# Attention scan with MoE on one core: another fixed table for the order of each engine's instructions

## The chip, the cores and the metric

The kernel runs on one core of one Trainium2 chip. The metric is the device time of one execution in microseconds (us). Five engines have an instruction queue of their own and work through it strictly in its order: TensorE (PE, with its weight loads PEld), VectorE (DVE), ScalarE (ACT), GpSimd (POOL) and SyncE (SP). SP issues every transfer (DMA) of this kernel. Where one engine needs another's result, or a transfer's, it waits at that instruction, and everything behind it in its queue waits too.

## The reference

Two stages. The first is a linear recurrence over 768 steps for 4 batches, 8 heads and 48 x 48 states, with a complex decay; the second is a feed-forward layer on 3072 tokens, 384 to 2048 and back.

```python
scale = np.minimum(mag, 0.999) / (mag + 1e-06)        # mag = |a|
for t in range(S):
    new_re = ar * S_re - ai * S_im
    new_im = ar * S_im + ai * S_re
    S_re, S_im = (new_re + k_t v_t^T, new_im)
    y[:, :, t] = q_t . S_re
h = x @ w_in                                          # x: y, heads side by side
g = h * np.tanh(softplus(h))
return g @ w_out
```

## The kernel before

The tokens are cut into 12 units of 256 (three to a batch, since the state S runs on from unit to unit within a batch), and each unit into two chunks of 128. A unit goes through three kinds of work.

- **Elementwise** (`ew_steps`, lines 341 to 530): the decays' magnitudes and angles are turned into running products. Tiles R and I hold the decay's real and imaginary part (loads at L358), QK holds q and k (loads at L365), X and X1 are work tiles. ACT squares, takes logarithms, exponentials and sines (L258 is a helper that records most of its operations, L278 the sines and L266 the change of its function table). DVE multiplies: L484 is QK times X, and the two at L505 write QK and X, which SP then turns into the tiles T (L501, twelve transfers a unit).
- **Attention of a chunk** (`attn_steps`): from unit 3 on, DVE transposes T into the tile vx (L586), SP writes vx to HBM as kd (L590), waits for that to land, and reads it back as three pieces of the tile kn (L592). PE then computes pd (L656) from kn and V, and DVE adds pd to the state S (L663, L664). PE computes the scores pa (L609), DVE masks them into am (L612, L616), and PE sums ypsum (L636) from am, V, vx, T and S. ACT copies ypsum to y (L641) and SP moves y into the layout of the second stage (xf, L690). There is one tile kn and one tile vx; V has two buffers.
- **Feed-forward** (`moe_steps`): 100 steps. In each, PE computes ph (L723, 18 matmuls), ACT makes exponentials and squares of it (e, L258), DVE clips (L728) and multiplies (g, L733), g is split into gh and gl (L290, L291), and PE accumulates po (L760, 12 matmuls). The results leave through o (L773, L775) and a write to out_dram (L776). The weights are converted and split in the first 165 us (raw, w). Lines L719 and L756 are the same two products for the first half steps. `spin` (L548) records 84 matmuls on junk data at the start.

What sets the order: nothing is left to a scheduler. `ORDER`, from line 74, holds one string of numbers for each of PE, Activation, Pool and SP, and one for DVE. The numbers count an engine's instructions in the order in which the program records them; `24+3` stands for 24, 25, 26. `in_order` ties each instruction to the one named before it. The buffers of every tile are handed out in the order of recording, so the tables don't touch them.

A number behind a name (X_2242) is that of the tile: R_1638, I_1639, X_2242, QK_2291 belong to unit 5, R_2243, I_2244, X_2817 to unit 6; kd4_1 is kd of unit 4, chunk 1.

Of the kernel before, what the change touches and what calls it, by code (L numbers as in the profile page):

```python
# [75 lines left out]
        0+24 40+4 48+8 44+4 56+8 24+8 64+16 32+4 124+4 36+4 128+8 80+12 188+3 226+3 92+4 248+3 191+3 229+3 136+4 251+3  # L76
        96+8 156+16 140+16 172+8 286+3 180+8 104+4 210+16 194+16 289+3 294+3 232+4 292+2 236+8 297+3 108+8 302+6 244+4
        254+32 116+4 300+2 310+6 308+2 318+3 120+4 321+3 316+2 326+18 324+2 348+9 344+4 368+9 357+9 377+9 366+2 408
        386+22 412+4 410 409 416+13 411 443 442 445 438+4 502+16 444 446+9 429+9 455+9 473 464+8 476+8 518+4 472 474
        484+18 522 475 530+18 568+9 523 526+4 524 577+9 525 606+9 560+8 586+8 548+6 615+9 557+3 597+3 636+9 554+3  # L80
        645+9 594+3 600+6 666+18 627+3 624+3 630+6 696+9 654+9 726+9 663+3 705+9 684+3 744+8 764+8 735+9 690+3 687+3
        693+3 714+6 776+9 720+6 755+3 834+18 785+9 752+3 761+3 825+3 758+3 822+3 831+3 896+18 828+3 950+9 868+6 959+9
        877+3 874+3 938+12 968+6 980 977+3 981+17 974+3 772 798+24 773+3 852+8 794+4 860+8 1018+18 998 880+16 914+24
        1001+3 999+2 1007+3 1047 1004+3 1044+3 1050+3 1048+2 1082+3 1010+8 1036+8 1088 1053+3 1085+3 1091+3 1056+18
        1102+9 1089+2 1111+9 1156+6 1144+3 1162+3 1147+3 1153+3 1185+3 1165+9 1202+9 1191+3 1211+5 1150+3 1216+4
        1182+3 1188+3 1120+24 1074+8 1094+8 1174+8 1240+18 1220+3 1226+3 1302+9 1266+3 1272+2 1194+8 1232+8 1278+24
        1258+8 1274 1223+3 1311 1229+3 1269+3 1275+3 1312+8 1332+18 1370+9 1323+3 1320+3 1326+3 1379+9 1350+3 1329+3
        1353 1356+2 1354+2 1408+18 1358+12 1400+8 1388+6 1397 1446+7 1508+9 1394+3 1453+11 1517+5 1398 1426+3 1399
        1432 1429+2 1522 1433+2 1431 1523+3 1472+3 1435+3 1554+9 1478+2 1475+2 1563+9 1477 1480+4 1584+9 1484+24
        1438+8 1464+8 1526+8 1546+8 1537+3 1534+3 1593+9 1540+2 1543+3 1542 1602+8 1622+8 1572+6 1630+9 1581+3 1578+3  # L90
        1639+9 1610+12 1648+2 1651 1660+18 1650 1654+3 1698+9 1652+2 1707+9 1657+3 1736+9 1681+3 1678+3 1745+9 1690+8
        1716+8 1687+3 1774+9 1828+3 1684+3 1831+4 1724 1835+2 1727+3 1725+2 1783+5 1730+3 1758+3 1837+5 1874+8 1788+4
        1733+2 1842+2 1735 1882 1761+3 1767+3 1764+3 1883 1844+2 1792+24 1884+3 1816+3 1887+5 1819+5 1825+3 1857
        1912+4 1858+2 1824 1754+4 1846+8 1770+4 1866+8 1916+5 1863+3 1854+3 1921+9 1860+3 1904+8 1950+24 1930+8 1974+9
        1892+9 1983+3 1901+3 1941+3 1986+6 1938+3 1947+3 1995+3 2004+18 2042+18 1944+3 2001+3 2025+3 2031+11 2060+8
        1992+3 2080+18 1998+3 2126+9 2071+3 2022+3 2135+9 2028+3 2068+2 2077+3 2180+8 2070 2188 2109+2 2074+3 2106+2
        2111 2108 2189+2 2098+8 2144+24 2198+8 2191+3 2112+2 2226+9 2194+4 2218+8 2118+8 2114 2235+7 2168+3 2174+3
        2115+3 2242+2 2206+3 2171+3 2264+9 2177+3 2209+3 2215+2 2273+9 2212+3 2217 2326+2 2256+8 2282+8 2328+7 2244+3
        2250+3 2290+3 2335+5 2247+3 2296+3 2253+3 2340+4 2293+3 2299+3 2356+17 2344+3 2350+3 2347+3 2373 2394+18
        2353+3 2374+6 2432+9 2383+2 2470+7 2385 2477+2 2441+9 2380+3 2479+5 2302+24 2386+8 2424+8 2412+5 2418+2 2417  # L100
        2420+4 2532+9 2453 2541+9 2484+4 2450+3 2454+2 2459+3 2456+3 2578+18 2508+24 2550+8 2462+8 2570+8 2488+11
        2502+3 2499+3 2505+3 2608+9 2558+3 2564+3 2561+2 2654+9 2626+8 2646+8 2563 2567+3 2596+3 2617+9 2602+3 2663+2
        2634+2 2665+7 2636 2599+3 2605+3 2640+3 2672 2637+3 2684+9 2643+3 2693+9 2722+9 2675+3 2673+2 2731+9 2681+3
        2678+3 2760+9 2702+3 2708+2 2705+2 2710 2748 2707 2711+3 2751+2 2749 2769+9 2714+8 2740+8 2798+9 2753 2750
        2852+4 2807+9 2757 2856+3 2758+2 2859+2 2754+3 2861 2782+2 2862+6 2785+3 2784 2898+10 2868+2 2791+3 2788+3
        2843 2908+2 2816+24 2778+4 2794+4 2870+8 2890+8 2840+3 2844+2 2910+5 2846+6 2915 2878+3 2936+9 2881+9 2945+9
        2998+9 2974+24 2928+8 2954+8 2916+3 3007+9 2922+3 2919+3 2925+3 2965+3 3028+9 2971+3 2962+3 3037+9 2968+3
        3016+3 3022+3 3019+2 3066+9 3021 3075+9 3025+2 3046+2 3104+10 3048 3114+6 3052+2 3027 3049+3 3055+3 3054
        3120+2 3150+17 3058+8 3084+14 3101+3 3204+8 3098+3 3133+3 3130 3250+11 3131+2 3139+2 3212+3 3167 3141 3261+6
        3215+2 3136+3 3192+6 3201+3 3217+5 3233+3 3198+3 3122+8 3168+24 3142+8 3222+8 3267 3230+3 3236+6 3288+16  # L110
        3350+4 3304+2 3354+5 3268+6 3277+3 3317+3 3242+8 3280+8 3326+24 3306+8 3274+3 3314+2 3380+5 3323 3385 3316
        3359+2 3324+2 3361+7 3320 3418 3371 3386+3 3419 3372+2 3389 3321+2 3390+8 3368+3 3420+4 3374+3 3398+3 3377+3
        3401+3 3424+3 3407+3 3427 3439 3404 3428+6 3405+2 3440+2 3434+5 3445+3 3410+8 3448+9 3494 3442+3 3474 3457+7
        3477+3 3475+2 3464 3495+2 3480+2 3465+9 3497+2 3556+7 3483+3 3482 3563+2 3499+13 3565+9 3520+6 3532+24 3486+8
        3574+8 3512+8 3594+8 3526+6 3602+2 3582 3604 3585 3632+5 3583+2 3586+2 3637+4 3605+6 3588+3 3678 3641 3611+8
        3591+3 3620+3 3619 3642+8 3626+3 3623+3 3679+5 3629+3 3684+3 3658+3 3687+9 3650+8 3670+8 3664+3 3696+3 3708+3
        3661+2 3702+3 3711+6 3738+8 3663 3746 3667+3 3699+3 3726 3717+2 3747+9 3719+7 3727+2 3732+3 3768+5 3705+3 3729
        3756 3773+4 3757+2 3762+3 3730+2 3735+3 3777+5 3759+3 3765 3798 3766+2 3782+4 3799+17 3789+2 3786+3 3828+9
        3792+3 3791 3795 3837+9 3796+2 3858+12 3816+3 3870+6 3822+3 3888+14 3819+3 3846+3 3825 3852+3 3918+4 3826+2
        3849+3 3855+3 3876+3 3902+4 3882+3 3906 3879+3 3885+3 3907+5 3922+5 3915+2 3912+2 3927+9 3917 3948+9 3914  # L120
        3957+9 4044 3978+8 3939+3 3945+3 3986+10 3969+3 3936+3 3942+3 3966+3 3972+3 3996+3 3975+3 3999+11 4011+3 4010
        4017+3 4014+3 4020+9 4032+6 4029+3 4038+6
    """,
    "DVE": """
# [890 lines left out]
```

## Time and profile before

| | us |
|---|---|
| median of 3 runs | 604.12 |
| lowest and highest of them | 603.61, 605.97 |
| the profiled execution, own time | 601.38 |
| its span, first to last instruction | 599.6 |

The profiled execution is the fastest of the four, 2.74 us (0.45%) under the median. PE is busy for 555.0 us of the span, DVE for 480.8, ACT for 484.3. A busy figure counts the time from an instruction's start to its end; matmuls overlap, so a PE that is busy in a whole stretch may still have lost time there, for example to a lower clock. PEclk, the granted clock of TensorE, is 1.00 at 2.4 GHz and 0.50 at 1.2 GHz. A releaser, the work named behind an arrow, is inferred from the semaphore that came last by the profile: where the engine named had long been done, it was another.

### The profile page before, as it was taken

How to read it: one execution, taken by the hardware profiler on the slowest of the kernel's cores; microseconds unless marked ns; L12 is line 12 of the kernel's file. 1: busy time of each engine (PE TensorE's matmuls, PEld its weight loads, DVE VectorE, ACT ScalarE, POOL GpSimd, SP SyncE). 2: the span in 40 equal slices, each digit the busy share in tenths (PEclk: the TensorE clock that was granted, in tenths of full speed). 3: DMA queues.
4: the chain of work that ended last, by engine and by line, in shares of the span. 5: the costliest groups of instructions: out<-in, count | busy, mean ns of one | idle time of the engine just before them, and what ended most of it. 6: DMA issues, size and time to landing. Idle time of an engine off the chain costs nothing.

```text
span 599.6 us, 13309 instructions
## 1 busy us (share of the span) xinstructions
PE 555.0 (93%) x5254; PEld 513.8 (86%) x5254; DVE 480.8 (80%) x865; ACT 484.3 (81%) x753; POOL 38.2 (6%) x58
## 2 busy tenths in 40 slices
PE   0878999999989989999899999899999999999995
PEld 0457777899989979999899899799989999999995
DVE  6989899999988968889878797797788887553542
ACT  7988999999876977999879888798788887455661
POOL 2112313230000000000000010000000000000000
PEclk9989999999999998999999999999999999999998
DMA  8787857324544835515817506527626524201000
GB/s 296 234 269 186 308 158 211 134 53 131 162 131 128 223 103 164 155 39 152 227 35 187 170 5 181 156 47 192 156 63 159 172 81 123 79 26 28 14 14 32
DMA packets 68041, 80.71 MB, mean 135 GB/s; under 512 B 5604, under 2 KB 60132, under 8 KB 67972
## 3 DMA queue, kind: packets, MB, share of 16 engines
q1 hardware_dynamic: 67972, 79.80, 45.9%
q8 instruction: 43, 0.70, 0.5%
q14 instruction: 26, 0.21, 0.1%
HBM read 44.63 MB, written 11.40 MB: 93 GB/s over the span
## 4 chain that ended last, share of the span: by engine, by line
PE 45%; DMA 19%; ACT 13%; DVE 13%; SPq 5%; issue 3%; DVEq 0%; ACTq 0%
PE po L760 17%; PE ph L723 15%; DMA kn<-kd 6%; ACT e L258 5%; DMA kd<-vx 5%; PE ypsum L636 4%; ACT X L258 2%; PE pa L609 2%; SPq L501 2%; PE pd L656 2%; PE junk L548 2%; PE ph L719 2%; PE po L756 2%; ACT L266 1%; SPq L592 1%
## 5 line engine op out<-in xcount | busy, mean ns | idle before, releaser
L723 PE MATMUL ph<-xH,w 128*128 128x256 f32 x1104 | 226.7, 287 | 2.6 <-DVE g L733 2.6
L760 PE MATMUL po<-w,gh 128*128 128x384 f32 x704 | 205.1, 341 | 0.2 <-DVE o L775 0.2
L723 PEld LDWEIGHTS ph<-xH,w 128*128 128x128 f32 x1104 | 181.3, 190 | 6.5 <-DVE g L733 2.8
L723 PE MATMUL ph<-xL,w 128*128 128x256 f32 x552 | 156.2, 283 | 0.6 <-DVE xL L291 0.6
L258 ACT ACTIVATE e<-e 128x512 f32<-128x512 f32 (+1 forms) x200 | 120.1, 610 | 26.1 <-DVE e L728 24.4
L760 PEld LDWEIGHTS po<-w,gh 128*128 128x128 f32 x704 | 130.3, 190 | 3.3 <-issue 1.8
L760 PE MATMUL po<-w,gl 128*128 128x384 f32 x352 | 118.9, 339 | 0.0
L723 PEld LDWEIGHTS ph<-xL,w 128*128 128x128 f32 x552 | 105.0, 190 | 2.4 <-DVE xL L291 0.8
L258 ACT ACTIVATE e<-ph 128x512 f32<-128x512 f32 (+1 forms) x100 | 57.3, 574 | 38.3 <-PE ph L723 34.9
L733 DVE SCALAR_TENSOR_TENSOR g<-e,ph 128x512 f32<-128x512 f32 (+1 forms) x100 | 66.0, 661 | 25.3 <-ACT e L258 16.4
L258 ACT ACTIVATE e<-e,fifth 128x512 f32<-128x512 f32 (+1 forms) x100 | 70.1, 702 | 1.3
L760 PEld LDWEIGHTS po<-w,gl 128*128 128x128 f32 x352 | 66.7, 190 | 0.2 <-DVE gl L291 0.2
L728 DVE TENSOR_SCALAR e<-e 128x512 f32<-128x512 f32 (+1 forms) x100 | 41.0, 411 | 30.7 <-ACT e L258 29.7
L291 DVE TENSOR_TENSOR gl<-g,gh 128x512 fp32r<-128x512 f32 x88 | 59.8, 682 | 4.8 <-ACT gh L290 4.5
L266 ACT ACT_TABLE_LOAD x47 | 60.3, 1283 | 1.6 <-PEq L971 0.8
L636 PE MATMUL ypsum<-am,V 128*48 128x128 f32 x240 | 37.0, 276 | 2.8 <-DVE am L616 2.4
L548 PE MATMUL junk<-cmask 128*128 128x512 bf16 x84 | 22.7, 418 | 14.4 <-DVE I L464 14.4
L324 POOL TENSOR_TENSOR raw<-raw 128x768 int32<-128x768 int32 x16 | 28.0, 1749 | 86.9 <-DVE raw L322 25.1
L258 ACT ACTIVATE X<-R 128x768 f32<-128x768 f32 (+1 forms) x40 | 30.0, 764 | 4.1 <-POOL X L488 2.0
L636 PE MATMUL ypsum<-T,S 96*48 96x128 f32 x320 | 33.1, 278 | 0.0
L258 ACT ACTIVATE X<-X 128x768 f32<-128x768 f32 (+1 forms) x42 | 31.2, 748 | 0.2
L656 PEld LDWEIGHTS pd<-V,kn 128*32 128x32 f32 (+2 forms) x880 | 18.0, 115 | 14.6 <-DMA kn<-kd 8.2
(93 smaller groups left out, 801.3 us busy)
## 6 DMA issues: line engine op xcount, KB each, us to landing
T<-X SPq DMA_DIRECT2D x72, 129.0 KB
T<-QK SPq DMA_DIRECT2D x72, 129.0 KB
raw<-w_in SPq DMA_DIRECT2D x8, 768.0 KB
raw<-w_out SPq DMA_DIRECT2D x8, 768.0 KB
kd<-vx SPq DMA_DIRECT2D x15, 384.0 KB
kn<-kd SPq DMA_DIRECT2D x45, 128.0 KB
V<-v SPq DMA_DIRECT2D x12, 384.0 KB
out_dram<-o SPq DMA_DIRECT2D x24, 192.0 KB
```

The lines of the kernel that those rows point to most:

```text
L258: ins = nc.scalar.activation(out, in_, func, **kw)
L266: ins = nc.scalar.preload_act_table_set(name)
L291: leng(out=lo, in0=src, in1=h.bitcast(F32), op=ALU.subtract)
L324: nc.gpsimd.tensor_tensor(hi, hi, lo, ALU.add)
L501: nc.sync.dma_start(rows[cs * NJ + j], src[:, c, j])
L548: ins = nc.tensor.matmul(junk, cmask, cmask.unsqueeze(1).broadcast_to([P, 4, P]), start=True, stop=True)
L636: nc.tensor.matmul(py[64 * par:64 * par + D, i, :], lhs, rhs, start=n == 0, stop=first or n == 1)
L656: nc.tensor.matmul(pd[lo:hi, h, :], knat[:, at0:at0 + hi - lo], own(c, h), start=not on_pe, stop=True)
L723: nc.tensor.matmul(ph[:, a, :], rows_in(parts[j][:, wp], kt, a), st[xp][:, kt, :], start=n == 0, stop=n == 8)
L728: nc.vector.tensor_scalar_min(e, e, math.exp(20.0))
L733: nc.vector.scalar_tensor_tensor(g, e, 2.5, ph, ALU.subtract, ALU.mult)
L760: nc.tensor.matmul(po[t], gp[:, a, tsl], rows_out(parts[NPAIR + j][:, wp], a), start=j in starts and a == 0 and n == 0, stop=j + 1 in ends ...
```

## The change

The strings of `ORDER` are replaced by others, for all five engines. They come from another run of the search that made the first ones, with transfers taken to land later than before. No operation, tile, buffer or transfer is added, removed or changed: each engine has the same instructions. The same 100 steps of the feed-forward stage follow each other on PE in the same sequence. What moves are the steps of the other two stages against them, by a few places mostly, and the transfers against each other. Of PE's table the first line was and is

```diff
     "PE": """
-        0+24 40+4 48+8 44+4 56+8 24+8 64+16 32+4 124+4 36+4 128+8 80+12 188+3 226+3 92+4 248+3 191+3 229+3 136+4 251+3
...
+        0+24 40+4 48+16 44+4 24+8 64+16 32+4 124+12 36+4 80+4 136+4 84+8 188+6 226+3 92+4 248+3 96+4 229+3 251+3
```

The first place is in unit 4's second chunk, at 206 to 231 us of the trace of before. On ACT, the square of unit 6's decay (X_2817<-I_2244) stood ahead of the sines of unit 5 (X1_2241, R_1638, L278):

```order
L258 ACTIVATE X_2242<-R_1638 128x6x128
L266 ACT_TABLE_LOAD
L641 COPY y_2316<-ypsum_100 112x4x128
L258 ACTIVATE X_2817<-I_2244 128x6x128
L278 ACTIVATE X1_2241<-I_1639 128x768
L278 ACTIVATE R_1638<-I_1639 128x768
L278 ACTIVATE R_1638<-R_1638,halfpi_93 128x768
L266 ACT_TABLE_LOAD
L258 ACTIVATE e_2499<-e_2499 128x512
```

It now stands behind them, and behind the next step's exponentials:

```order
L641 COPY y_2316<-ypsum_100 112x4x128
L266 ACT_TABLE_LOAD
L290 CAST gh_2348<-g_2346 128x512
L278 ACTIVATE R_1638<-I_1639 128x768
L278 ACTIVATE X1_2241<-I_1639 128x768
L258 ACTIVATE e_2499<-e_2499 128x512
L278 ACTIVATE R_1638<-R_1638,halfpi_93 128x768
L266 ACT_TABLE_LOAD
L258 ACTIVATE e_2499<-e_2499,fifth_97 128x512
L258 ACTIVATE e_2499<-e_2499 128x512
L258 ACTIVATE e_2557<-ph_2538 128x512
L641 COPY y_2316<-ypsum_100 112x4x128
L258 ACTIVATE X1_2816<-X_2817,tiny_95 128x768
L258 ACTIVATE X_2817<-I_2244 128x6x128
```

Where it followed the first copy of y_2316 at once, twelve instructions now stand between that copy and it. On SP, at the same place, the load of q for unit 5 (QK_2291<-q) stood behind all three pieces of kn, and the load of I_2244 among them:

```order
L365 DMA QK_2291<-k 128x6x128
L590 DMA kd4_1_2429<-vx_1633 96x1024
L592 DMA kn_102<-kd4_1_2429 128x1x256
L358 DMA I_2244<-a_im 128x768
L592 DMA kn_102<-kd4_1_2429 128x1x256 x2
L365 DMA QK_2291<-q 128x6x128
L776 DMA out_0_dram<-o_2463 128x384
L776 DMA out_0_dram<-o_2460 128x384
```

Now:

```order
L590 DMA kd4_1_2429<-vx_1633 96x1024
L365 DMA QK_2291<-q 128x6x128
L365 DMA QK_2291<-k 128x6x128
L592 DMA kn_102<-kd4_1_2429 128x1x256 x2
L776 DMA out_0_dram<-o_2460 128x384
L592 DMA kn_102<-kd4_1_2429 128x1x256
L358 DMA I_2244<-a_im 128x768
L776 DMA out_0_dram<-o_2463 128x384
```

Both loads of QK have moved ahead of the pieces of kn, I_2244 behind them, and a write of o_2460 stands before the last piece.

The second place is on DVE in unit 3, where vx_1633<-T_1395 is the transpose for the first chunk:

```order
L291 TENSOR_TENSOR gl_1670<-g_1667,gh_1669 128x512
L291 TENSOR_TENSOR gl_1727<-g_1724,gh_1726 128x512
L733 SCALAR_TENSOR_TENSOR g_1811<-e_1805,ph_1786 128x512
L455 TENSOR_TENSOR I_1127<-I_1127,X1_1636 128x3
L728 TENSOR_SCALAR e_1900<-e_1900 128x512
L291 TENSOR_TENSOR w11_1630<-raw11_550,w11_1630 128x768
L773 SCALAR_TENSOR_TENSOR o_1866<-po_1616,back_1864 128x384
L773 SCALAR_TENSOR_TENSOR o_1869<-po_1617,back_1864 128x384
L586 STREAM_TRANSPOSE vx_1633<-T_1395 96x8x4x32
```

Now:

```order
L733 SCALAR_TENSOR_TENSOR g_1811<-e_1805,ph_1786 128x512
L291 TENSOR_TENSOR w11_1630<-raw11_550,w11_1630 128x768
L290 CAST gh_1669<-g_1667 128x512
L586 STREAM_TRANSPOSE vx_1633<-T_1395 96x8x4x32
L291 TENSOR_TENSOR gl_1670<-g_1667,gh_1669 128x512
L728 TENSOR_SCALAR e_1900<-e_1900 128x512
L773 SCALAR_TENSOR_TENSOR o_1866<-po_1616,back_1864 128x384
L290 CAST gh_1813<-g_1811 128x512
L291 TENSOR_TENSOR gl_1727<-g_1724,gh_1726 128x512
```

The two gl, the clip of e_1900 and both o have moved from ahead of the transpose to behind it.

The third place is on SP in unit 9, first chunk, around kd9_0 and its three pieces of kn:

```order
L590 DMA kd9_0_4952<-vx_1633 96x1024
L501 DMA T_4884<-QK_4541 16x8x258
L592 DMA kn_102<-kd9_0_4952 128x1x256 x2
L365 DMA QK_5086<-q 128x6x128
L592 DMA kn_102<-kd9_0_4952 128x1x256
L501 DMA T_4884<-X_4500 16x8x258
L358 DMA R_5042<-a_re 128x768
```

Now:

```order
L590 DMA kd9_0_4952<-vx_1633 96x1024
L365 DMA QK_5086<-k 128x6x128
L592 DMA kn_102<-kd9_0_4952 128x1x256
L365 DMA QK_5086<-q 128x6x128
L592 DMA kn_102<-kd9_0_4952 128x1x256
L358 DMA R_5042<-a_re 128x768
L376 DMA vx_1633<-v 64x2x192
L592 DMA kn_102<-kd9_0_4952 128x1x256
```

Four loads that stood behind the last piece of kn, or one ahead of it, now stand between the landing of kd and that piece.

## Rows read from the trace of the kernel before

**Rows 1.** The page: busy; clock in 40 slices; a group (busy us, mean ns).

```profile
PE 555.0 (93%) x5254; PEld 513.8 (86%) x5254; DVE 480.8 (80%) x865; ACT 484.3 (81%) x753; POOL 38.2 (6%) x58
PEclk9989999999999998999999999999999999999998
...
L291 DVE TENSOR_TENSOR gl<-g,gh 128x512 fp32r<-128x512 f32 x88 | 59.8, 682 | 4.8 <-ACT gh L290 4.5
```

**Rows 2.** Waits of PE: waiting line <- releaser: total us, times, longest us.

```profile
PE junk L548 <- DVE I L464: 14.4, 1, 14.4
PE pd L656 <- DMA kn<-kd: 8.3, 9, 1.5
PE pkn L577 <- DMA T<-QK: 5.4, 3, 2.4
...
PE ypsum L636 <- DVE am L616: 2.4, 1, 2.4
```

**Rows 3.** Stretches: us, busy us (instructions) by engine, PEclk, DMA share, GB/s.

```profile
165.00:180.00 15.00, 13.02 (x96) 12.11 (x98) 12.14 (x22) 11.08 (x18) 1.02 (x2) 1.00 0.45 132
...
285.00:300.00 15.00, 12.70 (x127) 12.30 (x125) 12.31 (x24) 12.00 (x17) 0.58 (x2) 0.96 0.80 223
```

**Rows 4.** Timeline of PE: start us, us, what, count [idle before <-releaser].

```profile
221.65 0.87 PE L656 MATMUL pd<-V,kn 128*32 128x48 f32 x46 [1.01 <-DMA kn<-kd]
...
225.30 0.66 PE L636 MATMUL ypsum<-am,V 128*48 128x128 f32 x2 [2.42 <-DVE am L616]
```

**Rows 5.** Timeline of DVE, same columns.

```profile
222.84 1.76 DVE L484 TENSOR_TENSOR QK<-QK,X 128x1536 f32<-128x1536 f32 x1 [5.31 <-ACT R L278]
```

**Rows 6.** Timeline of ACT, same columns.

```profile
213.15 0.84 ACT L258 ACTIVATE X<-R 128x768 f32<-128x768 f32 x1
...
218.82 0.85 ACT L258 ACTIVATE X<-I 128x768 f32<-128x768 f32 x1 [2.94 <-DMA I<-a_im]
```

**Rows 7.** Timeline of SP's queue: start us, us of the issue.

```profile
206.66 0.34 SPq L590 DMA_DIRECT2D kd<-vx  x1
212.79 0.57 SPq L592 DMA_DIRECT2D kn<-kd  x1
...
215.07 0.79 SPq L365 DMA_DIRECT2D QK<-q  x1
```

**Rows 8.** Stretches of 4 us, columns as in rows 3.

```profile
224.00:228.00 4.00, 2.70 (x15) 2.24 (x16) 3.88 (x7) 1.90 (x4) 0.00 (x0) 0.50 0.12 45
228.00:232.00 4.00, 4.00 (x21) 4.00 (x20) 3.92 (x6) 2.81 (x5) 0.00 (x0) 0.68 0.51 134
```

**Rows 9.** Timeline of PE, units 3, 6 and 9, columns as in rows 4.

```profile
178.26 0.27 PE L656 MATMUL pd<-V,kn 128*32 128x48 f32 x2 [0.62 <-DMA kn<-kd]
179.86 0.87 PE L656 MATMUL pd<-V,kn 128*32 128x48 f32 x44 [1.32 <-DMA kn<-kd]
...
297.90 0.24 PE L656 MATMUL pd<-V,kn 128*32 128x48 f32 x2 [1.22 <-DMA kn<-kd]
299.24 1.49 PE L656 MATMUL pd<-V,kn 128*32 128x48 f32 x46 [1.09 <-DMA kn<-kd]
...
434.40 0.88 PE L656 MATMUL pd<-V,kn 128*32 128x48 f32 x48
```

**Rows 10.** Timeline of DVE, unit 3, columns as in rows 4.

```profile
166.75 1.00 DVE L773 SCALAR_TENSOR_TENSOR o<-po,back 128x384 f32<-128x384 f32 x2
```

**Rows 11.** Timeline of SP's queue, unit 9, columns as in rows 7.

```profile
424.71 0.55 SPq L592 DMA_DIRECT2D kn<-kd  x1
...
426.02 0.53 SPq L592 DMA_DIRECT2D kn<-kd  x1
```

**Rows 12.** Chain of waits in order of time: start us, us, what.

```profile
248.91 3.83 DMA QK<-q
...
290.87 8.32 DMA kn<-kd
...
515.96 5.17 DMA kn<-kd
```

More of the change, by code (lines that the diff above doesn't have):

```diff
@@ L75 @@
     "PE": """
[47 rows of a table removed]
[46 rows of a table added]
     """,
     "DVE": """
[29 rows of a table removed]
[29 rows of a table added]
     """,
     "Activation": """
[23 rows of a table removed]
[23 rows of a table added]
     """,
     "Pool": """
-        12+2 0 8 1 11 2+3 9 5+2 14 10 15+7 23 22 24+6 7 31 33 32 54 30 35 34 36+4 41 40 42+4 47 46 48+2 51 50 52+2
+        0 10 1 5 2 8 3 9 11 4 7 6 14+2 13 16 12 17+5 23 22 24+6 31 33 32 30 34 36 38+2 35 37 41 40 42+2 45 44 47 54 46
+        48+2 51 50 53 52
     """,
     "SP": """
[13 rows of a table removed]
[13 rows of a table added]
     """,
```

221 rows, old and new, of the table ORDER are left out of this document.

## Prediction

> **What bounds the kernel now.** The page's busy table comes first: PE is busy for 93% of the span, DVE and ACT for about 80% [rows 1]. So the time is PE's work plus what PE loses, and since no operation is changed, a table can only win back losses or add new ones. The second view is the list of what PE waited for [rows 2]. Its longest entry, 14.4 us, is the start: PE has nothing to do until the first angles are made. Behind it stand pd waiting for the read-back kn (8.3 us in 9 waits), pkn for the relayed T (5.4 us in 3) and one wait of ypsum for am (2.4 us). These 16.1 us, and what the clock loses after them, are about all that an order can win; the same list is the place where a worse table would show.
>
> The third view is the stretches, to see where the losses sit. At 165 to 180 us PE is busy for 13.0 of 15 us, at 285 to 300 for 12.7 [rows 3]. The worst place is 220 to 232 us. There pd waits 1.01 us for kn, then ypsum 2.42 us for am [rows 4], and the granted clock is 0.50 in the 4 us that follow and 0.68 in the next four [rows 8]: the lower of the two levels, 1.2 GHz.
>
> The fourth view is each engine's timeline there, followed back from am. DVE idles 5.31 us ahead of L484 [rows 5], so am, which stands behind it, is late. The row names ACT's sine R as releaser, but L484 is QK times X: it doesn't read R, and X's last exponential ended at 213.15 + 0.84 = 213.99 [rows 6]. What L484 also reads is the load of q, issued at 215.07 [rows 7], 7.77 us ahead of L484's start. I take that load as the true cause. It was late because SP's queue stood still: kd was issued at 206.66, the first piece of kn, which waits for kd's landing, at 212.79 [rows 7], and the load of q stood behind all three pieces. ACT has a stall of its own there: its square of the next unit's I waits 2.94 us for the load of I [rows 6], which stood between the same pieces, and unit 5's sines queue behind that square.
>
> **The change, part by part.** All sums are made against the profiled execution's own 601.38 us. The median of the runs is 604.12, 2.74 above it; I assume that distance to stay and carry the differences over to the median.
>
> *Unit 4, chunk 1.* Both loads of QK now stand directly behind kd instead of one behind the pieces of kn. If kd is issued as late as 2 us after 206.66, the load of q goes out by 210, 5 us earlier than at 215.07. With the same 7.77 us it lands by 217.8. DVE was ready for L484 at 222.84 - 5.31 = 217.53, so its stall falls from 5.31 to some 0.3 us. PE asked for am at 225.30 - 2.42 = 222.88; am is made some 2.5 us behind L484's start (225.30 - 222.84), so at 217.8 + 2.5 = 220.3. The wait of 2.42 us goes. ACT's square moves behind twelve instructions, sines and exponentials among them, so its load's lateness holds up neither the sines nor the step's exponentials: its 2.94 us are off the chain, and cost nothing more unless the load comes over 7 us later than those twelve allow. The clock: it is low from PE's restart at 225.30 to about 230.6 (4 us at 0.50 [rows 8], then (1 - 0.68) x 4 / 0.5 = 2.6 us), so 5.3 us of work at half speed, 2.6 us lost. It fell right behind this wait, so I let it go with it. The wait of 1.01 us for kn I leave: the pieces now stand behind two loads, and the last one behind a write of o_2460. Sum -2.4 - 2.6 = **-5.0**; bounds 0 (below) and -6.0 (with the 1.01).
>
> *Unit 3, chunk 0.* pd waits 0.62 + 1.32 = 1.94 us for kn [rows 9]. On DVE two gl (682 ns each by the page's group [rows 1]) and both o (1.00 us together [rows 10]) move from ahead of the transpose to behind it: 2.4 us. DVE is busy throughout there, so the transpose, kd and kn come up to 2.4 us earlier, and the wait is gone. The gl and o that now come later feed products several steps on; if that cover were gone, their 2.4 us would come back as a wait of po. **-1.9**; bounds 0 and -1.94.
>
> *Units 8 and 9.* In unit 9 the last piece of kn went out at 426.02, with the second at 424.71 and one load between [rows 11]: 0.65 us an issue. Now three more issues stand ahead of it, so it goes out some 2.0 us later, at 428.0. A piece took 5.17 to 8.32 us to land [rows 12], which gives 433.2 to 436.3, and PE took up pd at 434.40 [rows 9] without waiting: a new wait of 0 to 1.9 us. The piece is behind large loads, so the upper row is nearer; I take 1.0. Unit 8 has the same pattern, with more cover ahead of pd: 0.5. **+1.5**; bounds 0 and 3.8.
>
> For these pieces there is also a rule. The rows show the issues 0.65 us apart and no more: what a load ahead of a piece costs it in the transfer engines isn't to be seen in them apart. The Trainium skill, "DMA: Bandwidth & Descriptors", section "Queues, rings and completion order", says that each transfer engine consumes the descriptors of a ring in ring order, and that SP owns one row of rings. By it a piece would wait for all bytes ahead of it; the sum by the rows is the -5.4 below, by the rule it is the second rival's.
>
> *Unit 6* waits 1.22 + 1.09 us [rows 9] at a clock that falls too. Transpose and pd move later by about the same there: 0, bounds -3.8 and +1. *The other waits* for kn are 8.3 - 1.01 - 1.94 - 2.31 = 3.0 us, and pkn's 5.4 us belong to the first units, which alone use it and where the junk matmuls change places with the work: 0 for both, bounds -3 and +3, since I can't sign them by rows.
>
> Sum: -5.0 - 1.9 + 1.5 = **-5.4**: 601.38 - 5.4 = 596.0 in a profiled execution, 604.12 - 5.4 = **598.7** for the median.
>
> **The rivals.**
>
> *First: kn takes the wait that am leaves.* At the worst place PE stood at pd from 221.65 - 1.01 = 220.64, with the last pieces issued by 215.03. With two loads ahead (1.3 us) and the write of o_2460 to be waited for, the last one may go out 2.5 us later; pd then waits 3.5 us, the clock falls as before, and the 2.4 us of am are paid at pd instead. For it: SP's queue is strict, and DVE makes o_2460 only after other work. Against it: pd itself moves behind more products of the feed-forward stage. It gives 0 - 1.9 + 1.5 = -0.4: 603.7.
>
> *Second, the other side: loads ahead of kn are paid by their bytes.* A load of 384 KB takes 393 / 223 = 1.76 us at the 223 GB/s of a crowded stretch [rows 3]. In unit 9 two more stand ahead of the last piece (+3.5 us), in unit 8 three more (5.3, half of it covered: +2.6), in unit 4 two (+3.5, less am's 2.4: +1.1). One more fall of the clock, 2.6 us, comes with unit 9's wait. Sum 3.5 + 2.6 + 1.1 + 2.6 - 1.9 = +7.9: 612. It decides from the point where a piece takes longer than the 8.32 us that is the longest here. For it: 8.32 us stands for a piece behind loads, 5.17 us for one late in the kernel. Against it: a QK load alone took 3.83 us [rows 12], and in a queue that isn't full loads and pieces overlap. The page named above stands beside this one; it would make it the rule in every unit, and the rows' 8.32 against 5.17 bears it out only in part.
>
> *Third: the change doesn't do what it says.* The pieces might land no later than the first search assumed, the extra cover might fall on waits that weren't there, and each gain be matched by a new miss: 604.
>
> **How the numbers follow.** Forecast 0.58, first rival 0.24, second 0.13, third 0.05. The forecast's own range is 594.5 to 601. For 8 in 10 the range goes from 592.5, where unit 6, its clock and half of the unsigned waits go too (-5.4 - 3.8 - 2.4), to 607, which takes in the first and third rivals with 3 us of new waits and leaves the second out. About 0.5%, 3.0 us, is what a measurement of this kernel can tell from no change: faster than 601.1 has the forecast's 0.58, within has 0.29 (first and third), slower than 607.1 has 0.13.
>
> **What would show it.** In the new trace L484 of unit 5 starts without an idle time over 1 us, ypsum in unit 4 has no wait for am, and the granted clock between 210 and 240 us stays at 1.00. pd in unit 3 doesn't wait. In units 8 and 9 pd waits for kn by under 2 us each. A list of PE's waits with more than 8.3 us for kn speaks for the second rival; a pd wait of some 3 us near 222 us for the first. What would make the prediction wrong at once is a wait of PE of several us where before it had none, since PE is busy for 93% of the span and has no slack to pay it from.

## The result and the profile after

The changed kernel takes 579.16 us (median of four runs, 576.64 to 579.75), beside 603.87 us for the kernel before (602.16 to 605.97): a ratio of 0.958, interval 0.954 to 0.962. That is 24.7 us, where 5.4 were forecast, and it lies outside the range. The profiled execution took 578.97 us, with a span of 577.0. Medians and extremes, here and below, are over all runs; the ratios leave out the runs more than 1.5% above the fastest of their kernel.

The page of after, busy time and granted clock [rows 1]:

```profile
PE 547.6 (95%) x5254; PEld 509.5 (88%) x5254; DVE 480.8 (83%) x865; ACT 482.6 (84%) x753; POOL 39.7 (7%) x58
...
PEclk9899999999999999999999999999999999999999
```

The work is the same, the span shorter: PE's idle time fell from 44.6 us (599.6 - 555.0) to 29.4, and its busy time by 7.4 us. Part of that is the clock, which in this profile no longer drops between the start and the last matmul. It isn't all: with the order of before in all but one row, and no drop at all while PE works (e1_q_early, below), PE is still busy for 550.6 us, 3.0 more than here. What PE waited for, after [rows 2]:

```profile
PE junk L548 <- DVE I L464: 14.7, 1, 14.7
PE pd L656 <- DMA kn<-kd: 3.0, 3, 1.5
PE pkn L577 <- DMA T<-QK: 2.2, 2, 1.8
PE ph L723 <- DVE g L733: 1.2, 2, 0.8
```

Nine waits of pd for kn have become three, and the wait of ypsum for am (L616) is gone. Stretches of after [rows 3]; the middle one covers unit 4's second chunk:

```profile
165.00:180.00 15.00, 15.00 (x177) 14.23 (x178) 14.54 (x28) 12.99 (x20) 0.62 (x4) 1.00 0.34 109
210.00:225.00 15.00, 15.00 (x168) 14.50 (x168) 13.32 (x20) 14.38 (x22) 0.00 (x0) 1.00 0.52 141
285.00:300.00 15.00, 15.00 (x239) 14.12 (x238) 14.09 (x25) 13.61 (x22) 0.41 (x2) 1.00 0.31 103
```

PE is busy throughout, at the full clock. To see where the time went, PE's **loss** is followed along its work: the time less the sum of all matmuls so far, each at the usual distance between two starts at full clock (0.120 us in L723, 0.173 in L760; those of the small matmuls are estimates from the same traces, so a stretch can come out a little under zero). The stretches hold the same amount of PE's work in all kernels and are named by the time in the trace of before. "Mean" is over the profiles of this study with that order in that stretch. Some grafted orders (below) have their seam, where one order takes over from the other, inside a stretch and are counted there: at 184 us in unit 3 of after, at 268 in unit 4 and at 318 in unit 6 of before. The run that takes the order of before up again behind unit 3 (h_u3_only, loss 3.3) isn't in the mean of unit 4. Differences are taken before rounding.

| loss, us | before | after | mean, order of before | mean, order of after | difference of means | forecast |
|---|---|---|---|---|---|---|
| start, to 77 | 12.5 | 8.9 | 12.0 (10 profiles) | 10.5 (7) | -1.4 | 0 |
| to 160 | 3.3 | 3.8 | 3.3 (9) | 3.4 (6) | +0.1 | 0 |
| unit 3, to 212 | 2.3 | -0.4 | 2.7 (7) | -1.0 (7) | -3.7 | -1.9 |
| unit 4, to 289 | 6.7 | -0.3 | 6.3 (7) | -0.3 (4) | -6.6 | -5.0 |
| unit 6, to 334 | 4.3 | -0.8 | 3.4 (7) | -0.6 (5) | -3.9 | 0 |
| units 7 and 8, to 388 | 4.5 | 1.8 | 4.7 (9) | 2.3 (6) | -2.3 | +0.5 |
| the rest | 0.8 | -0.4 | 0.9 (11) | -0.6 (5) | -1.6 | +1.0 |

The means add up to -19.4 us. The whole change measured 24.7 in the first comparison and 21.4 in a second one (below). Some 1.2 us of the other 2 to 5 lie behind PE's work, where this loss doesn't look: from the start of PE's last matmul to the end of the span it takes 7.3 to 7.5 us in every profile that ends in the order of before, 5.9 to 6.4 in those that end in the order of after. The remaining 1 to 4 us aren't placed.

### The profile page after: what moved, and what is told of

It reads as the page before. It is cut to its first block, busy times and chain, and to the rows that moved or that the text cites. A ratio compares the mean times of both kernels' runs of the same rounds, so it can differ in the third digit from the quotient of the medians.

```text
span 577.0 us, 13326 instructions
## 1 busy us (share of the span) xinstructions
PE 547.6 (95%) x5254; PEld 509.5 (88%) x5254; DVE 480.8 (83%) x865; ACT 482.6 (84%) x753; POOL 39.7 (7%) x58
## 4 chain that ended last, share of the span: by engine, by line
PE 52%; DMA 6%; DVE 5%; SPq 3%; ACT 2%; issue 1%; DVEq 0%; ACTq 0%
PE po L760 22%; PE ph L723 21%; PE ypsum L636 4%; PE pa L609 3%; DMA kn<-kd 3%; PE pd L656 2%; SPq L501 2%; DMA kd<-vx 2%; ACT e L258 1%; DVE X L505 1%; DMA out_dram<-o 1%; DVE gl L291 1%; SPq L592 1%; DVE g L733 1%; ACT X L258 1%
## 5 line engine op out<-in xcount | busy, mean ns | idle before, releaser
L723 PE MATMUL ph<-xH,w 128*128 128x256 f32 x1104 | 225.7, 287 | 1.2 <-DVE g L733 1.2
L760 PE MATMUL po<-w,gh 128*128 128x384 f32 x704 | 202.3, 339 | 0.0
L723 PEld LDWEIGHTS ph<-xH,w 128*128 128x128 f32 x1104 | 180.7, 190 | 4.9 <-PE po L760 1.1
L723 PE MATMUL ph<-xL,w 128*128 128x256 f32 x552 | 156.0, 283 | 0.0
L258 ACT ACTIVATE e<-e 128x512 f32<-128x512 f32 (+1 forms) x200 | 119.7, 610 | 21.4 <-DVE e L728 19.6
L760 PEld LDWEIGHTS po<-w,gh 128*128 128x128 f32 x704 | 128.9, 188 | 2.4 <-issue 1.3
L760 PE MATMUL po<-w,gl 128*128 128x384 f32 x352 | 118.6, 337 | 0.8 <-DVE gl L291 0.7
L723 PEld LDWEIGHTS ph<-xL,w 128*128 128x128 f32 x552 | 104.7, 190 | 1.7 <-issue 0.6
L760 PEld LDWEIGHTS po<-w,gl 128*128 128x128 f32 x352 | 66.2, 188 | 1.4 <-DVE gl L291 1.3
L728 DVE TENSOR_SCALAR e<-e 128x512 f32<-128x512 f32 (+1 forms) x100 | 40.5, 409 | 16.5 <-ACT e L258 16.2
L548 PEld LDWEIGHTS <-cmask 128*128 128x128 bf16 x84 | 8.6, 106 | 23.9 <-issue 18.4
```

Of the source, the lines that this page charges most:

```text
L258: ins = nc.scalar.activation(out, in_, func, **kw)
L548: ins = nc.tensor.matmul(junk, cmask, cmask.unsqueeze(1).broadcast_to([P, 4, P]), start=True, stop=True)
L723: nc.tensor.matmul(ph[:, a, :], rows_in(parts[j][:, wp], kt, a), st[xp][:, kt, :], start=n == 0, stop=n == 8)
L728: nc.vector.tensor_scalar_min(e, e, math.exp(20.0))
L760: nc.tensor.matmul(po[t], gp[:, a, tsl], rows_out(parts[NPAIR + j][:, wp], a), start=j in starts and a == 0 and n == 0, stop=j + 1 in ends ...
```

## The experiments

Each ratio is to the kernel before on the same chip, with its 95% interval. For grafted orders "before until 188" means everything that had started by then in the trace of that kernel. There is one profile to a kernel: those of e1_q_early, e2_u6_pieces_first and b_pieces_first are of their fastest run, those of a4_q_late, a6_bulk_in_window and after_again of their slowest, so a loss read from one of them is not that of a typical run.

**The two loads in SP's queue, each alone.** First the load of q in unit 4:

```diff
 L590 DMA kd4_1_2429<-vx_1633 96x1024
+L365 DMA QK_2291<-q 128x6x128
 L592 DMA kn_102<-kd4_1_2429 128x1x256
...
-L365 DMA QK_2291<-q 128x6x128
```

> The kernel before, with one row of SP's queue moved: unit 5's load of q goes out directly behind the write of kd of unit 4, chunk 1, ahead of the three pieces of kn and the load of I; nothing else changes. My theory (the late load of q is what held am, 2.42 us of waiting and 2.6 us of low clock behind it): the load goes out near 207.0 instead of 215.07, L484 idles under 1 us instead of 5.31, the wait for am is gone, 599 to 601.5 us. Rival (kn takes the wait: the pieces go out behind one more load, pd waits 2 to 3.5 us instead of 1.01 and the clock falls as before): 603 to 605 us.

600.26 us, ratio 0.998 (0.9945 to 1.0019; ten runs from 593.74 to 603.88): no verdict by time. The trace shows the mechanism. L484 of unit 5 in this kernel [rows 5], on DVE, and then pd on PE [rows 4]:

```profile
215.73 1.76 DVE L484 TENSOR_TENSOR QK<-QK,X 128x1536 f32<-128x1536 f32 x1
```

```profile
219.61 0.87 PE L656 MATMUL pd<-V,kn 128*32 128x48 f32 x46 [0.63 <-DMA kn<-kd]
```

L484 has no idle time ahead of it, ypsum doesn't wait for am, pd waits no longer than before, and unit 4's loss is 3.0 instead of 6.7. The reverse is clearer, since the runs of after lie closer together. The kernel after with that row put back:

```diff
 L590 DMA kd4_1_2429<-vx_1633 96x1024
-L365 DMA QK_2291<-q 128x6x128
 L365 DMA QK_2291<-k 128x6x128
...
 L592 DMA kn_102<-kd4_1_2429 128x1x256
+L365 DMA QK_2291<-q 128x6x128
 L358 DMA I_2244<-a_im 128x768
```

> The kernel after, with one row of SP's queue put back: unit 5's load of q goes out behind the three pieces of kn of unit 4, chunk 1, instead of ahead of them. Theory (the load's lateness held am before): it goes out near 210.5 instead of 203.3 and lands near 216.5, L484 starts some 4.5 us later than 212.0 and DVE idles there; the time is 2 to 5 us above that of after. Rival (the orders of PE and DVE that came with it have taken the cover over): within 1 us of after.

583.38 us (581.17 to 586.62) beside 580.18 (577.55 to 582.58) for after in the same comparison; ratios 0.969 (0.964 to 0.974) and 0.963 (0.958 to 0.968), whose intervals overlap. Its DVE and its PE:

```profile
218.36 1.76 DVE L484 TENSOR_TENSOR QK<-QK,X 128x1536 f32<-128x1536 f32 x1 [4.20 <-DMA QK<-q]
```

```profile
220.82 0.42 PE L636 MATMUL ypsum<-am,V 128*48 128x128 f32 x2 [2.75 <-DVE am L616]
```

One late load brings back DVE's stall, now with the load itself as its releaser, the wait for am, and a clock of 0.79 from 220 to 228 us; unit 4's loss rises by 4.8. In the trace the theory holds and the rival doesn't; by time, the 3.2 us lie in the theory's range but aren't clear of the spread.

Then unit 6, which the prediction had put at 0. SP's queue there in the kernel before [rows 7 are of unit 4]:

```profile
282.97 0.33 SPq L590 DMA_DIRECT2D kd<-vx  x1
283.35 0.55 SPq L501 DMA_DIRECT2D T<-QK  x1
283.99 0.58 SPq L376 DMA_DIRECT2D vx<-v  x1
...
285.26 0.61 SPq L376 DMA_DIRECT2D vx<-v  x1
285.92 0.77 SPq L501 DMA_DIRECT2D T<-X  x1
286.79 0.52 SPq L358 DMA_DIRECT2D I<-a_im  x1
287.36 1.50 SPq L371 DMA_DIRECT2D V<-v  x1
288.96 0.59 SPq L365 DMA_DIRECT2D QK<-k  x1
289.60 1.77 SPq L592 DMA_DIRECT2D kn<-kd  x3
```

and in the kernel after:

```profile
273.61 0.34 SPq L590 DMA_DIRECT2D kd<-vx  x1
276.42 0.59 SPq L365 DMA_DIRECT2D QK<-k  x1
277.51 1.18 SPq L592 DMA_DIRECT2D kn<-kd  x2
278.73 0.47 SPq L371 DMA_DIRECT2D V<-v  x1
279.25 0.52 SPq L592 DMA_DIRECT2D kn<-kd  x1
```

Before, eight transfers, five of them loads (two halves of vx, I, V, k), stand between kd and its first piece, which goes out 6.6 us behind kd. After, one does, and it is 3.9 us. By the landing times in the traces kd itself lands 3.8 and 3.9 us behind its issue, so 2.8 of the 6.6 us are the queue's. The kernel before with only that changed:

```diff
 L590 DMA kd6_0_3269<-vx_1633 96x1024
 L501 DMA T_3201<-QK_2858 16x8x258
-L376 DMA vx_1633<-v 64x2x192
-L501 DMA T_3201<-X_2817 16x8x258
-L376 DMA vx_1633<-v 64x2x192
-L501 DMA T_3201<-X_2817 16x8x258
+L501 DMA T_3201<-X_2817 16x8x258 x2
+L592 DMA kn_102<-kd6_0_3269 128x1x256 x3
+L376 DMA vx_1633<-v 64x2x192 x2
 L358 DMA I_3360<-a_im 128x768
 L371 DMA V_3286<-v 128x768
 L365 DMA QK_3403<-k 128x6x128
-L592 DMA kn_102<-kd6_0_3269 128x1x256 x3
```

> The kernel before, with SP's queue of unit 6, chunk 0 in another order: the five bulk loads (two halves of vx, I, V, k) that stood between the write of kd and the three pieces of kn go out behind the pieces. Nothing else changes. Theory of bulk in the way: the last piece lands about 5 us earlier than 299.2, pd's waits of 1.22 and 1.09 us go and with them the fall of the clock (1.7 us): 599 to 601 us. Rival (the loads are only late elsewhere: V, I, k come 3 to 5 us later and hold the next unit as long): 603 to 606 us.

598.83 us, ratio 0.995 (0.991 to 0.999). Both waits are gone, and the loss in unit 6 is 0.4 instead of 4.3. Its PE [rows 9]:

```profile
297.04 0.88 PE L656 MATMUL pd<-V,kn 128*32 128x48 f32 x48
```

The reverse, in the kernel after, with R in the place of V and k:

```diff
+L590 DMA kd6_0_3269<-vx_1633 96x1024
+L376 DMA vx_1633<-v 64x2x192 x2
 L358 DMA I_3360<-a_im 128x768
 L358 DMA R_3359<-a_re 128x768
...
-L590 DMA kd6_0_3269<-vx_1633 96x1024
```

> The kernel after, with SP's queue of unit 6, chunk 0 undone: four bulk loads (two halves of vx, I, R) go out behind the write of kd and ahead of the pieces of kn again, where the kernel after has them ahead of kd. Nothing else changes. Theory of bulk in the way: the last piece lands 4 to 5 us later than 286.1, pd waits 2.5 to 3.5 us more, and with the clock the time is 3 to 6 us above that of after: 582 to 585 us. Rival (the order of PE, DVE and ACT has given unit 6 the cover, and the place of the loads doesn't matter): within 1 us of after.

581.27 us (579.99 to 581.71), ratio 0.968 (0.964 to 0.972). pd's wait is back, but only

```profile
289.22 0.87 PE L656 MATMUL pd<-V,kn 128*32 128x48 f32 x46 [0.94 <-DMA kn<-kd]
```

and the loss in unit 6 rises by 1.2, to 0.4. Neither theory's number is met: the place of the loads matters, but it costs a third of what moving them gained in before. The landing times tell why. PE gets to pd 13.6 to 13.7 us behind the issue of kd in all four kernels, so its cover is the same. The last piece lands 16.2 us behind kd in before, 11.3 with the pieces ahead of the loads, 12.5 in after and 14.8 here. Not all of that is a later issue: from its own issue to its landing the last piece takes 8.3, 6.5, 6.9 and 8.1 us.

**SP's queue alone, at five places.**

```diff
 L590 DMA kd3_0_1730<-vx_1633 96x1024
 L365 DMA QK_1678<-q 128x6x128
+L592 DMA kn_102<-kd3_0_1730 128x1x256 x3
 L376 DMA vx_1633<-v 64x2x192 x2
-L592 DMA kn_102<-kd3_0_1730 128x1x256 x3
...
 L590 DMA kd7_0_3836<-vx_1633 96x1024
+L592 DMA kn_102<-kd7_0_3836 128x1x256 x3
 L365 DMA QK_3974<-k 128x6x128
-L592 DMA kn_102<-kd7_0_3836 128x1x256 x2
 L371 DMA V_3853<-v 128x768
-L592 DMA kn_102<-kd7_0_3836 128x1x256
 L365 DMA QK_3974<-q 128x6x128
+L590 DMA kd7_1_4112<-vx_1633 96x1024
...
+L592 DMA kn_102<-kd7_1_4112 128x1x256 x3
```

> The kernel before, with SP's queue alone changed by one rule at six places: no bulk load (vx, V, R, I, q, k) and no relay stands between the write of kd and its three pieces of kn, and kd goes out as soon as the transpose is made (unit 3 chunk 0; unit 6 chunk 0; unit 7 both chunks), and the load of q in unit 4 stands behind kd. The instructions of PE, DVE and ACT keep the order of before. Theory that SP's queue makes most of the gain: PE's loss falls by 3.8 us in unit 4 and 3.9 in unit 6, as when each was moved alone, and by 1 to 4 us more in units 3 and 7: 590 to 594 us beside 602 for before. Rival (the order of the three engines makes the gain; moved loads come back as waits elsewhere): 597 to 602 us.

594.56 us, ratio 0.989 (0.983 to 0.996): 6.1 us by the medians, just short of the theory's range. The edit changes five places, not six, and keeps the rule only in part: the load of q still stands between kd and its pieces in units 3 and 4, that of I between the pieces in unit 4, three T in unit 6 and five transfers in unit 7's second chunk. SP's queue at these places makes between a quarter and a third of the gain by itself, going by the middle of an interval from 2.6 to 10.5 us. Unit 3 kept its waits (0.97 and 0.99 us): its last piece lands 10.9 us behind kd, as in before, and PE gets to pd 8.5 us behind it.

**Unit 3: the prediction's second term by itself.**

```diff
-L291 TENSOR_TENSOR gl_1670<-g_1667,gh_1669 128x512
-L291 TENSOR_TENSOR gl_1727<-g_1724,gh_1726 128x512
 L733 SCALAR_TENSOR_TENSOR g_1811<-e_1805,ph_1786 128x512
...
+L586 STREAM_TRANSPOSE vx_1633<-T_1395 96x8x4x32
+L291 TENSOR_TENSOR gl_1670<-g_1667,gh_1669 128x512
+L291 TENSOR_TENSOR gl_1727<-g_1724,gh_1726 128x512
 L773 SCALAR_TENSOR_TENSOR o_1866<-po_1616,back_1864 128x384
 L773 SCALAR_TENSOR_TENSOR o_1869<-po_1617,back_1864 128x384
-L586 STREAM_TRANSPOSE vx_1633<-T_1395 96x8x4x32
```

> The kernel before, with unit 3, chunk 0 alone changed: DVE makes the transpose of k ahead of two gl and both o instead of behind them, and SP writes kd ahead of the output. This is the term of -1.9 us of the prediction by itself. Theory: kd goes out 2.4 us earlier, pd's two waits of 0.62 and 1.32 us go, 1.9 us under before, 3.5 with the fall of the clock that some profiles show at 176 to 184 us: 597 to 599.5 us beside 601 for before. Rival (the gl and o that come later are waited for by po, or the pieces are held by the loads between them and not by the transpose): within 1 us of before.

601.34 us, ratio 0.999 (0.995 to 1.003). pd doesn't wait for kn in unit 3 any more, but PE has a new wait:

```profile
170.66 0.45 PE L760 MATMUL po<-w,gh 128*128 128x384 f32 x1 [2.23 <-DVE o L773]
```

The wait was moved from pd to po, as the rival said. Nor did the transpose come 2.4 us earlier. On DVE in this kernel, and then in before:

```profile
165.71 0.69 DVE L733 SCALAR_TENSOR_TENSOR g<-e,ph 128x512 f32<-128x512 f32 x1 [0.83 <-ACT e L258]
...
167.71 1.24 DVE L586 STREAM_TRANSPOSE vx<-T 96x1024 f32<-96x1024 f32 x1
```

```profile
167.68 1.23 DVE L586 STREAM_TRANSPOSE vx<-T 96x1024 f32<-96x1024 f32 x1
```

This run is already 1.1 us behind at L441, ahead of these rows, so by the work the transpose comes some 1 us earlier. Where the two gl had stood, DVE now idles 0.83 us for ACT's e. pd finds its pieces there because PE comes to it 3.3 us later, 2.23 of them spent on the wait for o. Then unit 3 with all five engines' new order:

```diff
-the order of before throughout
+before until 130 us, after until 184 us, before for the rest
```

> The order of before up to 130 us, that of the kernel after for all that it has started by 184 us (unit 3), and the order of before from there, on all five engines. Theory that PE's own order supplies the cover which the transpose moved alone lacked: pd in unit 3 chunk 0 doesn't wait and po doesn't wait for o either, 2 to 3.5 us under before: 597.5 to 599.5 us beside 601. Rival (the wait is only moved, as in the run with the transpose alone, or comes back at the seam): 600 to 603 us.

595.38 us, ratio 0.988 (0.979 to 0.997): 6.9 us, twice the theory. Neither pd nor po waits in unit 3 (loss -1.0). PE gets to pd 10.5 us behind the issue of kd there instead of 8.4 in before, and the last piece lands 10.4 us behind it: so it is mainly the order of the engines, not the queue, that ends the wait. The rest of the gain lies one unit on. There ypsum waits 1.17 us for am instead of 2.42, the clock stays up, and unit 4's loss is 3.3. So what unit 3 wins isn't only its own.

**Single stretches and halves.** In the same way, with the diff's second line as named:

```diff
-the order of before throughout
+before until 188 us, after until 231 us, before for the rest (h_u4_only)
+before until 268 us, after until 292 us, before for the rest (h_u6_only)
+before until 318 us, after until 375 us, before for the rest (h_u78_only)
+after until 82 us, before for the rest (h_head_only)
+after until 258 us, before for the rest (a_until_258)
+before until 268 us, after for the rest (a_from_268)
```

> The order of the kernel before up to 188 us, that of the kernel after for all that it has started by 231 us (unit 4, both chunks), and the order of before from there, on all five engines. Theory that each stretch's gain belongs to the stretch's own order: PE's loss between units 3 and 5 falls by the 6.3 us that the two traces show there, 597 to 599 us. Rival (the gain needs the lead that the engines bring from the earlier stretches): a gain of 0 to 3 us, 601 to 604 us.

596.13 us, ratio 0.989 (0.981 to 0.996): 6.9 us by the ratio, 5.4 by the medians; the time lies just under the theory's range. The loss in unit 4 is 0.6, as in the theory.

> The order of the kernel before up to 268 us, that of the kernel after for all that it has started by 292 us (unit 6), and the order of before from there, on all five engines. Theory that each stretch's gain belongs to its own order: the 5.6 us that the traces show there, 597.5 to 600 us. Rival (the gain needs the lead from earlier stretches): 602 to 605 us.

600.98 us, ratio 0.996 (0.992 to 1.000), between the two ranges. The loss in unit 6 is 0.4, as in the theory, but units 7 and 8, in the order of before, lose 7.1 in this profile where the mean is 4.7, with the clock down at 376 to 388 us.

> The order of before up to 318 us, that of the kernel after for all that it has started by 375 us (unit 7 and the first chunk of unit 8), and the order of before from there, on all five engines. Theory that the new order wins there, too, against the prediction's loss of 0.5: 2 to 3 us under before, 598 to 599 us beside 601, and pd waits under 1 us in unit 8. Rival (the loads ahead of the pieces in unit 8 cost what the prediction took, or the lead is lost at the seam): 600.5 to 602 us.

600.89 us, ratio 0.997 (0.993 to 1.001): no gain by time, and the time lies in the rival's range. In the trace the loss in units 7 and 8 is 1.0 instead of 4.5. pd in unit 8 doesn't wait, as in before; in unit 7's second chunk it still waits 1.75 us for kn.

> All five engines in the order of the kernel after for what it has started by 82 us, then in the order of before. Theory that the start gains too, which the prediction put at 0: PE's loss in the first 50 us of its work is 1 to 3 us smaller, 598 to 600 us beside 601 for before. Rival (the spread of the first transfers from run to run makes the difference between the two traces): within 1 us of before.

599.15 us, ratio 0.996 (0.992 to 1.000). The start's loss of 11.3 lies within the 10.0 to 13.3 of the profiles with the order of before, so a gain of a few us by time isn't placed by the trace.

> All five engines in the order of the kernel after for what it has started by 258 us (units 0 to 5), then in the order of before. Theory that the gain is local and adds up: the loss that the traces show for after up to there is some 13 us under that of before, of which the start's 2.8 may be chance, so 589 to 592 us beside 602 for before. Rival (a table is one whole, the later part of before can't use the lead or loses it at the seam): 594 to 602 us.

593.50 us, ratio 0.990 (0.982 to 0.997). Units 3 and 4 gain nearly what they gain in after (losses -1.0 and 1.0), but unit 6, in the order of before, loses 6.6 instead of 4.3: the seam gives part of the lead back. The time lies 1.5 us above the theory's range and just under the rival's.

> All five engines in the order of before for what it has started by 268 us, then in the order of the kernel after. Theory that the gain is local and adds up: 3.3 us in unit 6 and some 5 us in units 7 to 11: 593 to 595 us beside 602 for before, and this gain and that of the run with the first part sum up to the whole change's 22. Rival (the later part needs the lead of the first): 598 to 602 us.

592.25 us, ratio 0.987 (0.983 to 0.991): 7.8 us by the ratio; the time lies 0.75 us under the theory's range. The five single stretches add up to some 20 us by their ratios (0.4, 1.2, 1.1, 0.4 and 0.3% of 602), close to the whole, though each is uncertain by 2 to 5 us; the two halves add up to 14, less than their parts and less than the 22 of the expectation. With 5 and 2 us of interval on the halves neither sum is sharp, so whether the gain is a sum of local gains isn't shown.

**After again, and a better table.**

```diff
 the kernel after, unchanged
```

> The kernel after, unchanged, beside the two kernels that differ from it by rows of SP's queue, and a second profile of it. Both theories: 0.95 to 0.97 of before. If the drops of the clock are a matter of chance, its losses at units 3, 4 and 6 still stay as small as in the first profile (under 1 us each).

580.18 us, ratio 0.963 (0.958 to 0.968). Its losses in units 3, 4 and 6 are as small as in the first profile. Unit 7's isn't (below). The first profile of after still shows pd waiting for kn at three places, in units 7 and 9. The same rule was applied there:

```diff
+L590 DMA kd7_0_3836<-vx_1633 96x1024
+L501 DMA T_3768<-X_3358 16x8x258
+L592 DMA kn_102<-kd7_0_3836 128x1x256 x3
 L358 DMA R_3926<-a_re 128x768
...
 L590 DMA kd7_1_4112<-vx_1633 96x1024
+L592 DMA kn_102<-kd7_1_4112 128x1x256 x3
...
 L590 DMA kd9_0_4952<-vx_1633 96x1024
+L592 DMA kn_102<-kd9_0_4952 128x1x256 x3
 L365 DMA QK_5086<-k 128x6x128
-L592 DMA kn_102<-kd9_0_4952 128x1x256
```

> The kernel after, with SP's queue alone changed where its trace still shows pd waiting for kn: in unit 7 chunk 0 and unit 9 chunk 0 kd goes out first and the pieces of kn directly behind it, ahead of the loads of R, k, q and vx; in unit 7 chunk 1 the pieces go out directly behind kd instead of 19 us later. Theory (what stands in front of the pieces makes the wait): the three waits of 0.90, 1.50 and 0.63 us go, 575 to 577.5 us if after is at 579. Rival (the loads that come later are missed as long, or SP stands still for kd while others wait behind it): 578 to 582 us.

576.06 us (574.93 to 578.89), ratio 0.959 (0.955 to 0.963), beside 580.18 for after in the same comparison: 4.1 us less, though the intervals overlap a little. What PE waits for in it:

```profile
PE junk L548 <- DVE I L464: 14.3, 1, 14.3
PE pd L656 <- ACT kn L578: 2.5, 2, 2.2
PE pkn L577 <- DMA T<-QK: 2.0, 2, 1.4
PE ypsum L636 <- DVE am L623: 2.0, 3, 1.1
```

The kn of the second row is the one that ACT copies in the first units. No wait for a piece that is read back is left. This is the fastest of the kernels here.

## Why the prediction was wrong, step by step

- **What bounds the kernel**: right in the main. PE's work is fixed, and what changed is its waits and the clock behind them. But of the 16.1 us that I called about all that an order can win, 5.2 are still there in after (3.0 for kn, 2.2 for T), and PE's idle time fell by 15.2 us and its busy time by 7.4: there was more to win than those rows show.
- **Unit 4, -5.0**: right in its mechanism, a little small (-6.6). The late load of q held L484 and by it am; by the trace of before the load lands at 222.77 us, 0.07 ahead of L484's start; moving it alone ends that in the trace, putting it back brings it again. The wait of 1.01 us for kn went too in after, which was the term's bound of -6.0.
- **Unit 3, -1.9**: the size was half of what came (-3.7), and the reason was incomplete. I let the transpose move past 2.4 us of DVE's work, because DVE was busy throughout, and called the cover of gl and o given, with the price of a lost cover beside it. But the two gl had filled a wait of DVE for ACT: moved alone, the transpose comes only about 1 us earlier, and nearly the whole price is paid: po waits 2.23 us. With all engines' order nobody waits. That it is PE's own order which supplies the cover is the likely reading; PE's order alone wasn't tried.
- **Unit 6, 0**: this is the step that failed most. I compared the places of the transpose and of pd, saw both move by about the same, and signed it 0 with a bound of -3.8. Both do move together (pd comes 13.6 to 13.7 us behind kd in either kernel). What mattered stood between them, in SP's queue: those five loads between kd and its pieces. They could be counted in the table before the run, as in unit 4. Moving them alone in before took the loss from 4.3 to 0.4.
- **The other waits, 0 with bounds of 3**: units 7 and 8 gained 2.3, the start about 1.4 and the rest 1.6. Summed with unit 6 this is 9 us put at nothing for want of a sign. Unit 6's bound was near the truth; setting all the middles to 0 was the mistake. Even so it isn't only a matter of the middles: all bounds together (-6.0, -1.94, 0, -3.8, and -3 for each of the two other waits) reach -17.7, and 21 to 25 us came. By the means units 3 and 4 went past their bounds, and the stretches with units 8 and 9, signed as a loss, gained.
- **Units 8 and 9, +1.5**: unit 8 has no wait in after, unit 9 one of 0.64 us in the first profile and 0.14 in the second, where 1.0 was put. The mechanism, loads ahead of a piece, is real, and b_pieces_first takes the wait away by moving them.
- **First rival**: fell. pd doesn't wait in unit 4 of after.
- **Second rival**: its mechanism is the right one and its sign was wrong. A piece does pay for what stands ahead of it, by unit 6 in both directions. But in units 4 and 6 it is the table of before with which the last piece lands late (15.0 and 16.2 us behind kd, against 12.2 and 12.5 in after). The loads alone don't give the sign: counted over all fifteen kd, 20 loads stand between kd and its last piece in before and 24 in after, and the three more of them in unit 8 cost no wait in after. The 3.83 us that I read as a load alone are only its share of a chain: it stood among the pieces and landed 4.78 us behind its issue. The Trainium skill, "DMA: Bandwidth & Descriptors", section "Queues, rings and completion order", says that each transfer engine takes the descriptors of a ring in ring order; unit 6 agrees, where the last piece takes 6.5 us from its issue to its landing ahead of the loads and 8.3 behind them, and pd's waits of 1.22 and 1.09 us end. I had read the rule for the two units where the new table adds loads, and not for unit 6, where it takes them away.
- **The clock**: I let it go with unit 4's wait, and it went; in unit 6 I had it in the bound alone. Behind the waits of units 3, 6 and 7 it falls in some runs and not in others (last section), so a wait that goes there saves more on average than its own length.

## What to carry to other kernels

When a table of an order changes, ask two things of every wait for a transfer, in both tables: what stands in the issuing queue between that transfer's input and the transfer itself, and how much work the busiest engine has between that input and its use. Unit 6 changed by the first alone, unit 3 by the second; neither gives the sign without the other. A transfer that the busiest engine waits for goes ahead of bulk loads that nobody needs soon. Terms that can't be signed one by one still add up: if all come from the same rule, their middles are not 0 together. And one instruction moved ahead on one engine can hand its wait to the next consumer; here only the new order of all engines had the cover for it.

## What the runs showed of the hardware

The clock's fall behind a wait isn't the same from run to run. In unit 3, with the same order, pd waits twice for kn. Here is PE and the granted clock when unit 6 alone was changed (e2_u6_pieces_first; columns as in [rows 9] and [rows 3]):

```profile
178.83 0.27 PE L656 MATMUL pd<-V,kn 128*32 128x48 f32 x2 [0.51 <-DMA kn<-kd]
180.41 0.87 PE L656 MATMUL pd<-V,kn 128*32 128x48 f32 x44 [1.31 <-DMA kn<-kd]
```

```profile
180.00:184.00 4.00, 3.59 (x93) 3.35 (x94) 2.51 (x6) 1.00 (x2) 0.00 (x0) 1.00 0.11 38
```

and in the run with the order of after from 268 us on (a_from_268, whose line numbers are higher by one):

```profile
178.56 0.27 PE L657 MATMUL pd<-V,kn 128*32 128x48 f32 x2 [0.41 <-DMA kn<-kd]
180.04 0.87 PE L657 MATMUL pd<-V,kn 128*32 128x48 f32 x44 [1.20 <-DMA kn<-kd]
```

```profile
180.00:184.00 4.00, 3.96 (x84) 3.90 (x85) 2.23 (x6) 0.31 (x1) 0.00 (x0) 0.66 0.12 36
```

The waits are even a little shorter in the second, and the clock fell. In unit 6, with the order of before there, pd waited 1.22 and 1.09 us in before [rows 9], and the clock fell:

```profile
300.00:304.00 4.00, 4.00 (x46) 3.88 (x38) 2.99 (x5) 2.69 (x6) 0.31 (x1) 0.72 0.21 65
```

In h_u3_only it waited no less,

```profile
290.13 0.24 PE L657 MATMUL pd<-V,kn 128*32 128x48 f32 x2 [1.51 <-DMA kn<-kd]
291.29 0.87 PE L657 MATMUL pd<-V,kn 128*32 128x48 f32 x46 [0.91 <-DMA kn<-kd]
```

and the clock stayed at 1.00 from 288 to 300 us. In unit 4 it was not so: in all seven profiles with the order of before in unit 4's second chunk and ypsum's wait of 2.4 to 2.5 us for am, the clock fell to the lower level there. The two profiles of after differ in the same way at unit 7, where the first waits 1.50 us and the clock stays up, while the second waits longer:

```profile
362.79 1.50 PE L656 MATMUL pd<-V,kn 128*32 128x48 f32 x48 [2.44 <-DMA kn<-kd]
```

Its clock is 0.50 in the four us from 364, and units 7 and 8 lose 5.1 us instead of 1.8. That is a likely reason why the runs of before spread over 7 to 10 us within each of the later comparisons, and the six of b_pieces_first, with no wait for kn, over 4. The runs' own clocks speak for it, without showing which wait it was: of the 69 runs of before that count for the ratios there, the 14 with a mean granted clock of 0.980 or less have a median of 604.19 us, the 9 with 0.991 or more one of 599.25. The mean is 0.985 for these runs of before and 0.994 for the eight of after; on some 600 us that is an estimate of 5 to 6 us, about a quarter of the gain, that comes by the clock.
